# The last two result tiles of a routed mixture of experts: turned by TensorE and stored as whole rows

## The chip, the cores and the metric

The kernel runs on one core of one Trainium2 chip. The core has five engines that run at the same time and meet only at semaphores: TensorE (PE in the profile, and PEld for its weight loads), VectorE (DVE), ScalarE (ACT), GpSimd (POOL) and SyncE (SP). SP computes nothing; it issues DMAs. ACT can issue DMAs too. The DMAs of both queues run on the core's 16 DMA engines. The metric is the device time of one execution in microseconds, lower is better. A time is given as the median over several executions.

## The reference

Two blocks in a row. The first is an attention with a polynomial sketch (4 batches, 4 heads, 1088 positions, 32 dimensions for each head); its output, heads side by side, is the matrix x of 4352 tokens by 128 features. The second sends x through 8 experts, and its result is a weighted sum over all of them:

```
logits = x @ w_gate
P = np.exp(logits - logits.max())
for _ in range(8):
    P /= P.sum(1, keepdims=True) + 1e-09
    P /= P.sum(0, keepdims=True) + 1e-09
    P *= N / E
for e in range(E):
    h = np.maximum(x @ w1[e], 0.0)     # 128 -> 1024 features
    out += P[:, e:e + 1] * (h @ w2[e]) # 1024 -> 128 features
```

Everything is float32. The output has 4352 rows of 128 numbers, 512 bytes for each token.

## The kernel before

Features lie on the 128 partitions and tokens along the columns, so xT holds x turned round. The columns are not in the order of the tokens: each batch has 34 blocks of 32 columns, and column 32a + s of a batch is token 34s + a. Blocks that follow each other in the columns are therefore rows that follow each other in the output, and the 32 columns of one block are rows that lie 34 rows apart.

The expert part is cut into groups of tokens (`groups`, L644 to L653) and, in a group, into items, one for each expert. TensorE makes the hidden features of 256 tokens at a time (`first`, L920), ScalarE applies the maximum with zero, and TensorE multiplies by w2 (`into`, L1092), into four PSUM banks that the program names s. To spare products, blocks of w2 and of the hidden features are added and subtracted beforehand, so that a bank holds no finished output; finished tiles come from sums of banks, which VectorE makes (`part_of_seven`, `part_of_twenty`, and `last_part` for the last group).

The last group is `(0, 256, 2, [2..7], True)`: two tiles of 256 tokens, columns 0 to 511 of batch 0. `last_part` (L795) is called when a bank of this group is complete, in the order 3, 0, 2, 1. Bank 2 completes the tile y2 (columns 256 to 511), bank 1, the last, completes the tile y1 (columns 0 to 255). From two blocks before the end on, the order on VectorE, TensorE and ScalarE is the order in which the program issues the instructions (`manual_schedule`, L1126). The products of bank 1 are the last ones on TensorE.

A finished tile has features on partitions and tokens in columns, and the output wants tokens in rows. `put` (L723) has VectorE transpose the tile in squares of 32 by 32 (L726). Partition 32r + s of the result holds, for every block of the tile, the 32 features of quarter r of one token. `store` (L878) then issues four DMAs, one for each quarter r; each writes 32 times 8 pieces of 32 numbers, which are 128 bytes, a quarter of a row (L884). In the last group the four alternate between the queues of SP and ACT:

```
            for r in range(4):
                queues[r % len(queues)].dma_start(
                    out=AP(tensor=out.tensor, offset=out[b * S + a, 32 * r].offset,
                           ap=[[SA * DM, 32], [DM, m], [1, 32]]),
                    in_=yt[32 * r:32 * (r + 1), b0 - first:b0 - first + m, :])
```

All other groups store by `put` as well, with SP alone, in the middle of the program. Other names that matter here: `bank()` (L94) gives one of four PSUM banks named a, which `first` uses; `ident` (L286) is the 128 by 128 identity in SBUF, which `routing` (L597) and `kept_to_sums` (L1060) use as an operand; L630 stores the routing weights, four DMAs of 8 rows each, into a DRAM tensor pT; L191 loads w2 in pieces of 512 bytes; line L1280 is where the program ends and the engines meet.

Of the kernel before, what the change touches and what calls it, by code (L numbers as in the profile page):

```python
# [10 lines left out]
F32 = mybir.dt.float32  # L11
# [39 lines left out]
def kernel(  # L51
# [12 lines left out]
    nc = tc.nc  # L64
    P = nc.NUM_PARTITIONS
    B, H, S, D = q.shape
    R = S1.shape[0]
    N, DM = out.shape
# [3 lines left out]
    SA = S // 32  # L72
# [6 lines left out]
    H2 = DM // 2  # L79
# [14 lines left out]
    def bank():  # L94
        return aps.tile([P, 512], F32, tag="a", name="a")
# [61 lines left out]
    loaded, pools = {}, []  # L157
# [128 lines left out]
    ident = consts.tile([P, P], F32, name="ident")  # L286
# [436 lines left out]
    def put(y, lo, n, queues):  # L723
        b0, nb = lo // 32, n // 32
        yt = pools[0].tile([P, NT3 // 32, 32], F32, tag="yt", name="yt", bufs=4)[:, 0:nb, :]
        nc.vector.transpose(out=yt.rearrange("p b d -> p (b d)"), in_=y)  # L726
        store(yt, b0, b0 + nb, queues)

    def part(g, k):

        if g in DIRECT:
            lo, n, _, es, _ = groups[g]
            nc.scalar.copy(kept[es[0]][:, lo + k * n:lo + (k + 1) * n], sums[g][k])
        elif groups[g][2] == 3:
            part_of_twenty(g, k)
        elif g < len(groups) - 1:
            part_of_seven(g, k)
        else:
            last_part(g, k)
# [47 lines left out]
    def last_rooms(g):  # L787
        n = groups[g][1]
        own = parts.setdefault(g, {})
        if not own:  # L790
            own.update(y=[pools[0].tile([P, NT3], F32, name=f"y{t}", bufs=1)[:, 0:n] for t in range(2)],
                       **{a: room(a, n) for a in "zwxfr"})
        return [own[a] for a in "yzwxfr"]

    def last_part(g, k):  # L795


        lo, n, *_ = groups[g]
        s0, s1, s2, s3 = sums[g]

        def add(out, a, b):
            nc.vector.tensor_tensor(out, a, b, op=Alu.add)

        (y1, y2), z, w, x, f, r = last_rooms(g)
        if k == 3:
            nc.scalar.copy(r[upper], s3[lower])
            add(w[upper], s3[upper], r[upper])
        elif k == 0:
            nc.scalar.copy(z[upper], s0[lower])
            nc.scalar.copy(f, s0)  # L810
            add(x[upper], z[upper], w[upper])
            add(z[upper], x[upper], s0[upper])
        elif k == 2:
            nc.scalar.copy(r[lower], s2[upper])
            nc.scalar.copy(x[lower], s0[lower])
            add(y2[upper], z[upper], s2[upper])
            add(y2[lower], s2[lower], r[lower])
            add(x[upper], x[upper], s2[upper])
            put(y2, lo + n, n, (nc.sync, nc.scalar))
        else:  # L820
            add(y1, s1, x)
            put(y1, lo, n, (nc.sync, nc.scalar))

    def part_of_twenty(g, k):

# [52 lines left out]
    def store(yt, b0, b1, queues):  # L878
        first = b0
        while b0 < b1:  # L880
            b, a = divmod(b0, SA)
            m = min(b1 - b0, SA - a)
# [5 lines that stand above are left out]
            b0 += m  # L888
# [396 lines left out]
```

## Time and profile before

| what | us |
|---|---|
| median of 6 runs | 920.09 (919.62 to 921.14) |
| the profiled execution | 919.79 |
| its span, first to last instruction | 918.0 |
| PE busy in the span | 911.1 (99%) |
| DVE busy | 689.3 (75%) |
| ACT busy | 421.2 (46%) |
| POOL busy | 211.9 (23%) |
| last matmul begins and ends its group | 911.07 to 913.00 |
| last DMA issue begins, on SP and on ACT | 914.92 and 914.96 |

The profile is one execution. The rows of a timeline give the start in microseconds from the span's start, how long the row took, the engine, the line of the program, the operation with its tiles (out<-in) and shapes, and how many instructions are merged in the row. An engine name with a q at its end (SPq, ACTq) is that engine's queue, where DMAs are issued. The row of an issue is over before the data move. In a table of stretches, "DMA share" is the mean busy share of the 16 DMA engines, from the time that their packets took, and can be over 1 where packets of one engine overlap. A DMA has one packet for each contiguous piece that it moves, and beside these some packets of 4 bytes, here called marks, that tell the semaphore that a part has landed; each of the last eight stores has 256 packets and 16 marks.

### The profile page before, as it was taken

The page shows a single profiled execution, that of the slowest core. Times are in us where ns is not written, and L with a number is a line of the kernel's source. Part 1 is how long each engine was busy: PE and PEld are TensorE (multiplying, and loading weights), DVE is VectorE, ACT ScalarE, POOL GpSimd, SP SyncE. Part 2 cuts the span into 40 slices and gives each one's busy share as a digit, 9 for nine tenths or more (in the row PEclk, how much of TensorE's full clock was granted, in tenths as well). Part 3 has the DMA queues.
Part 4 walks back from the last instruction along what each step waited for, and adds up shares of the span by engine and source line. Part 5 has one row for each costly group of instructions (what it writes and reads, how often), then busy time and mean ns, then how long its engine had stood idle before and what let it go on. Part 6 is the DMA issues. An engine that isn't in the chain of part 4 may idle for free.

```text
span 918.0 us, 18917 instructions
## 1 busy us (share of the span) xinstructions
PE 911.1 (99%) x7450; PEld 594.6 (65%) x7450; DVE 689.3 (75%) x1173; ACT 421.2 (46%) x915; POOL 211.9 (23%) x220
## 2 busy tenths in 40 slices
PE   9999999999999999999999999999999999999997
PEld 7877544466666666666666666666666655556886
DVE  8678699888877798766975666966567976658665
ACT  3455555554444454444544444544445444445443
POOL 5121100175555421201210010110100243211220
PEclk9999999999999999999999999999999999999999
DMA  9994100214453535434363343453334455453640
GB/s 260 315 269 155 54 1 1 70 64 140 144 162 119 187 119 172 166 110 150 114 186 132 119 141 112 134 186 128 132 123 165 131 169 196 161 166 93 173 155 13
DMA packets 91305, 128.15 MB, mean 140 GB/s; under 512 B 25392, under 2 KB 69504, under 8 KB 86480
## 3 DMA queue, kind: packets, MB, share of 16 engines
q1 hardware_dynamic: 88384, 121.42, 41.9%
q0 software_dynamic: 1600, 5.36, 1.9%
q8 instruction: 58, 0.95, 0.4%
q10 hardware_dynamic: 1232, 0.16, 0.1%
q14 instruction: 31, 0.25, 0.1%
HBM read 107.88 MB, written 19.05 MB: 138 GB/s over the span
## 4 chain that ended last, share of the span: by engine, by line
PE 98%; DVE 1%; issue 0%; ACT 0%; POOL 0%; DVEq 0%; POOLq 0%
PE a L926 56%; PE s L1111 38%; PE a L352 1%; PE a L474 1%; PE a L114 1%; PE a L319 0%; DVE hb L943 0%; PE s L381 0%; PE a L438 0%; PE s L404 0%; PE a L508 0%; PE a L387 0%; PE a L404 0%; DVE cs L614 0%; DVE rs L608 0%
## 5 line engine op out<-in xcount | busy, mean ns | idle before, releaser
L926 PE MATMUL a<-xe,w 128*64 128x256 f32 (+1 forms) x2560 | 663.3, 470 | 0.0
L926 PEld LDWEIGHTS a<-xe,w 128*64 128x64 f32 x2560 | 300.7, 137 | 105.8 <-issue 1.6
L1111 PE MATMUL s<-hb,ws 128*64 128x256 f32 (+3 forms) x1312 | 314.0, 395 | 0.2 <-DVE hb L943 0.2
L930 ACT ACTIVATE hb<-a 128x256 f32<-128x256 f32 (+4 forms) x408 | 194.8, 480 | 242.0 <-PE a L926 209.0
L1111 PE MATMUL s<-hx,ws 128*64 128x256 f32 x1280 | 289.2, 379 | 0.0
L930 ACT ACTIVATE hx<-a 128x256 f32<-128x256 f32 (+1 forms) x360 | 167.1, 464 | 213.7 <-PE a L926 193.9
L990 DVE TENSOR_TENSOR hb<-hb 128x512 f32<-128x512 f32 (+1 forms) x204 | 139.4, 693 | 97.9 <-ACT hb L930 93.8
L990 DVE TENSOR_TENSOR hx<-hx 128x512 f32<-128x512 f32 (+1 forms) x204 | 154.8, 769 | 60.6 <-ACT hx L930 55.4
L1111 PEld LDWEIGHTS s<-hb,ws 128*64 128x64 f32 x1312 | 148.7, 137 | 77.6 <-issue 26.1
L690 POOL TENSOR_TENSOR xe<-xT,xe 128x768 f32<-128x768 f32 (+2 forms) x41 | 82.5, 2014 | 480.6 <-DMA xe<-pT 398.5
L1111 PEld LDWEIGHTS s<-hx,ws 128*64 128x64 f32 x1280 | 145.8, 137 | 62.4 <-issue 13.4
L1111 PE MATMUL s<-hb,w 128*64 128x256 f32 (+3 forms) x536 | 129.0, 408 | 0.0
L926 PE MATMUL a<-xT,w 128*64 128x416 f32 (+3 forms) x512 | 120.2, 462 | 0.0
L1111 PE MATMUL s<-hx,w 128*64 128x256 f32 x384 | 90.4, 379 | 0.0
L943 DVE TENSOR_TENSOR hb<-hb 128x416 f32<-128x416 f32 (+7 forms) x84 | 60.2, 717 | 20.5 <-ACT hb L930 16.6
L1111 PEld LDWEIGHTS s<-hb,w 128*64 128x64 f32 x536 | 57.9, 137 | 23.4 <-issue 6.6
L926 PEld LDWEIGHTS a<-xT,w 128*64 128x64 f32 x512 | 50.1, 137 | 24.3 <-issue 15.3
L242 POOL TENSOR_TENSOR ws<-w 128x256 f32<-128x256 f32 (+1 forms) x70 | 63.3, 938 | 5.8 <-DMA w<-in_moe_w_dram 4.4
L943 DVE TENSOR_TENSOR hx<-hx 128x256 f32<-128x256 f32 (+1 forms) x65 | 39.5, 612 | 24.3 <-ACT hx L930 23.1
L1111 PEld LDWEIGHTS s<-hx,w 128*64 128x64 f32 x384 | 44.1, 137 | 11.4
L990 DVE TENSOR_TENSOR pqg<-hb 128x512 f32<-128x512 f32 x68 | 45.3, 708 | 0.0
L990 DVE TENSOR_TENSOR pqg<-hx 128x512 f32<-128x512 f32 x68 | 34.7, 551 | 0.0
(184 smaller groups left out, 485.2 us busy)
## 6 DMA issues: line engine op xcount, KB each, us to landing
w<-in_moe_w_dram SPq DMA_DIRECT2D x82, 512.0 KB, 5.5
ws<-ws SPq DMA_DIRECT2D x34, 1024.0 KB, 5.0
xe<-pT SPq DMA_DIRECT2D x34, 384.0 KB, 3.9
ws<-ws SPq DMA_DIRECT2D x12, 512.0 KB, 4.0
ph<-qa SPq DMA_DIRECT2D x12, 288.0 KB, 4.9
rb<-qb SPq DMA_DIRECT2D x3, 1152.0 KB, 6.5
pb<-pT SPq DMA_DIRECT2D x6, 384.0 KB, 7.5
kx<-in_k_dram SPq DMA_DIRECT2D x4, 544.0 KB, 4.0
```

What stands on the lines that cost most here:

```text
L114: nc.tensor.matmul(warm[:, 0:P], ones, ones, start=True, stop=True)
L242: tc.keep_in_program_order(nc.gpsimd.tensor_tensor(ws[:, c:c + len(ns)], blocks(x), blocks(y), op=Alu.subtract if off else Alu.add))
L352: nc.tensor.matmul(pv[64 * s:64 * (s + 1), i], kp[0:n, H * t + h].rearrange("p i j -> p (i j)"), vx[0:n, slots[h], t, :], start=(t == 0 an ...
L474: nc.tensor.matmul(pn[64 * s:64 * (s + 1), t, 2 * i:2 * i + 2].rearrange("p h d -> p (h d)"), ph[:, i, s, 64 * t:64 * (t + 1)], kvs[b % 2] ...
L690: tc.keep_in_program_order(nc.gpsimd.tensor_tensor(out, x, pb, op=Alu.mult))
L926: nc.tensor.matmul(ph[sl], loaded_w[j][0][:, P * f + H2 * s:P * f + H2 * (s + 1)], sources[j][:, lo:hi], start=True, stop=True, tile_posit ...
L930: nc.scalar.activation(out=out, in_=ph, func=Act.Relu)
L943: nc.vector.tensor_tensor(out, a, b, op=Alu.subtract)
L990: nc.vector.tensor_tensor(out if not isinstance(out, tuple) else places(*out), places(*a), places(*b) if isinstance(b, tuple) else b, op=A ...
L1111: nc.tensor.matmul(sums[g][i][H2 * s:H2 * (s + 1), n * place:n * (place + 1)], w, x, start=c == 1, stop=c == per, tile_position=(0, H2 * s))
```

## The change

In `last_part`, bank 2 no longer calls `put` for y2. When bank 1 is complete, y1 is added in two halves of 128 columns. Then each of the four pieces of 128 tokens (two of y2, two of y1) is turned by TensorE: the piece is the stationary operand, 64 columns at a time, the identity is the moving operand, and the two products fill a 128 by 128 corner of a PSUM bank with tokens on partitions and all 128 features along the columns. ScalarE copies the pieces of y2 to SBUF, VectorE those of y1. Four DMAs, alternating between SP and ACT, write 128 rows of 512 bytes each. Their output pattern counts, from the slowest to the fastest, 4 blocks, 32 rows that lie 34 rows apart, and 128 numbers.

```
--- before.py
+++ after.py
@@ -816,10 +816,27 @@
             add(y2[upper], z[upper], s2[upper])
             add(y2[lower], s2[lower], r[lower])
             add(x[upper], x[upper], s2[upper])
-            put(y2, lo + n, n, (nc.sync, nc.scalar))
         else:
-            add(y1, s1, x)
-            put(y1, lo, n, (nc.sync, nc.scalar))
+
+            rows = [slice(P * i, P * (i + 1)) for i in range(n // P)]
+            for c in rows:
+                add(y1[:, c], s1[:, c], x[:, c])
+            work_ = [(y, first_ + c.start, y[:, c]) for y, first_ in ((y2, lo + n), (y1, lo)) for c in rows]
+            turned_ = []
+            for _, _, y in work_:
+                pt = bank()[:, 0:P]
+                for i in range(2):
+                    sl = slice(H2 * i, H2 * (i + 1))
+                    nc.tensor.matmul(pt[sl], y[:, sl], ident, start=True, stop=True, tile_position=(0, H2 * i))
+                turned_.append(pt)
+            for i, (y, token, _) in enumerate(work_):
+                yt = pools[0].tile([P, P], F32, name=f"row{i}", bufs=1)
+                (nc.scalar.copy if y is y2 else nc.vector.tensor_copy)(yt, turned_[i])
+                b, a = divmod(token // 32, SA)
+                (nc.sync, nc.scalar)[i % 2].dma_start(
+                    out=AP(tensor=out.tensor, offset=out[b * S + a, 0].offset,
+                           ap=[[DM, P // 32], [SA * DM, 32], [1, DM]]),
+                    in_=yt)
```

## The prediction

> **What bounds the kernel now.** First the page's busy times and the chain that ended last: TensorE is busy all the time, so all but the last few microseconds are its own work, which the change leaves alone.
>
> ```profile
> span 918.0 us, 18917 instructions
> PE 98%; DVE 1%; issue 0%; ACT 0%; POOL 0%; DVEq 0%; POOLq 0%
> ```
>
> So only the end matters, and there I read the timeline, from the last products on:
>
> ```profile
> 911.07 1.93 PE L1111 MATMUL s<-hb,w 128*64 128x256 f32 x15
> ...
> 912.15 0.42 DVE L802 TENSOR_TENSOR y<-s,r 64x256 f32<-64x256 f32 x1
> 912.60 0.42 DVE L802 TENSOR_TENSOR x<-x,s 64x256 f32<-64x256 f32 x1
> 913.05 0.45 DVE L726 STREAM_TRANSPOSE yt<-y 128x256 f32<-128x256 f32 x1
> 913.52 1.84 SPq L884 DMA_DIRECT2D out_dram<-yt  x4
> 913.53 0.42 DVE L802 TENSOR_TENSOR y<-s,x 128x256 f32<-128x256 f32 x1
> 913.53 1.91 ACTq L884 DMA_DIRECT2D out_dram<-yt  x4
> 913.99 0.45 DVE L726 STREAM_TRANSPOSE yt<-y 128x256 f32<-128x256 f32 x1
> ```
>
> The reader is to see that computing is over at 914.44, and that the first stores are issued at 913.52. The other 3.6 us are DMA. The table of short stretches shows of what kind:
>
> ```profile
> 914.30:914.40 0.10, 0.00 (x0) 0.00 (x0) 0.10 (x1) 0.00 (x0) 0.00 (x0) 1.00 0.10 15
> 914.50:915.00 0.50, 0.00 (x0) 0.00 (x0) 0.00 (x0) 0.00 (x0) 0.00 (x0) 1.00 0.91 133
> 915.50:916.00 0.50, 0.00 (x0) 0.00 (x0) 0.00 (x0) 0.00 (x0) 0.00 (x0) 1.00 0.90 132
> 916.40:916.50 0.10, 0.00 (x0) 0.00 (x0) 0.00 (x0) 0.00 (x0) 0.00 (x0) 1.00 0.18 23
> ```
>
> The last two columns are the DMA share and GB/s. Data begin at 914.38, some 0.86 us after the first issue, and all 16 engines are about 0.9 busy until 916.5. The stores queue at the engines: the end is set by the first issue, 0.86 us, the time the engines need for all packets, and about 1.5 us from the last packet to the end of the span at 918.0 (the last marks land, SP sees them, the engines meet). Each term is judged by this.
>
> **The change part by part.** *Taken away:* two transposes on DVE (2 x 0.45 us), eight issues (0.34 to 0.47 us each), and 2048 packets of 128 bytes. In place of them come 512 packets of 512 bytes.
>
> *Added for y2.* y2 is ready at 912.57, but TensorE runs in order and ends its last products at 913.00. A product of the same shape stands in `routing`:
>
> ```profile
> L597 PE MATMUL a<-ident,mx x4: 272/272/273, 114.4 to 115.2; 128*64 128x128 f32 x4
> L810 ACT COPY f<-s 128x256 f32<-128x256 f32 x1 | 0.4, 372 | 0.0
> L830 ACT COPY z<-s 128x512 f32<-128x512 f32 x5 | 2.9, 583 | 0.0
> ```
>
> A pair runs side by side on two halves of the array, so the first piece is in PSUM by 913.27. A copy of 128 columns on ACT takes half the step from 512 to 256 columns less than 372 ns: 372 - 106 = 266 ns, so 913.55. The first issue on SP is then at about 913.57, today 913.52. I take the start of data as unchanged, 914.4. The second copy puts the first ACT issue at 913.85.
>
> *Added for y1.* With the transpose of y2 gone, the addition starts at 913.05. DVE takes 0.42 us for 256 columns and 0.69 us for 512 (the subtractions of hx just before the end), so 0.29 us for 128: halves at 913.34 and 913.66. Then 0.14 us of weight load, 0.27 us of product and 0.29 us of copy: the last issue, on ACT, at 914.45. The granted clock is 1.00 here. The new waits (PE for DVE, ACT and DVE for PE, the queues for the copies) have nothing queued behind them but the next piece and the program's end. All four stores are at the DMA engines by 915.3, so nothing of this shows as long as the engines are then still working off earlier stores; where they are not, it is the path, as in the rival with 16 engines.
>
> *The stores.* Here I differ from what the packet sizes alone suggest. How many engines a store uses can be read where a store has few rows. L630 writes four times 8 rows; the stretch from 171.2 to 174.0 has it:
>
> ```profile
> DMA packets 57, 0.15 MB, mean 53 GB/s; under 512 B 24, under 2 KB 24, under 8 KB 56
> q1 hardware_dynamic: 56, 0.14, 36.1%
> pT<-qT SPq DMA_DIRECT2D x4, 34.0 KB
> ```
>
> 56 packets are 4 x 8 rows and 24 marks of 4 bytes. Three stores had ended, so each left 8 marks and ran on 8 engines. Today's final stores, whose slowest dimension counts 32, leave 2176 packets, which is 8 x (256 + 16): all 16 engines. The new pattern counts 4 in its slowest dimension on the DRAM side, against 128 partitions on the other. No row here has two sides that differ below 16; the bounds are 4 engines and 16. I take 4, by the pT rows, in which the slowest dimension set the number.
>
> [...]
>
> *Pace.* On 4 engines each store is 32 packets for one engine, and all four go to the same engines one after the other: in the pT stretch four separate bursts follow each other too. For a packet of 512 bytes the loads of w2 are the nearest rows (stretches 820 to 825 and 822.5 to 823.0):
>
> ```profile
> q1 hardware_dynamic: 1040, 0.52, 38.5%
> ...
> q1 hardware_dynamic: 341, 0.17, 115.1%
> ```
>
> The first gives 0.385 x 5 us x 16 / 1040 = 30 ns a packet, the second, at full flow, 0.5 us x 16 / 341 = 23.5 ns from one packet to the next: the lower end. The upper end is pT again: 0.361 x 2.8 x 16 / 32 = 0.50 us a packet of 4352 bytes, where a load of k (0.956 x 0.6 x 16 / 50, from 3.5 to 4.1) took 0.18 us. Few engines on neighbouring partitions cost 2.7 times there, which would be 80 ns. I take 30 / 0.9 = 33 ns, since today's stores keep an engine 0.9 busy: near the lower end, because the new stores read all 128 partitions, not 8 adjacent ones.
>
> [...]
>
> *Sum.* 4 stores x (32 x 33 ns + 10 ns for a mark) = 4.26 us. Start 914.4 + 4.26 + 1.5 = 920.16, against 918.0: **+2.1 us**. The profiled execution (919.79) would be 921.9. The median of the six runs stands 0.3 above it, so I forecast 920.09 + 2.1 = **922.2 us**. At 23.5 ns it is 914.4 + 3.05 + 1.5 = 918.95 (+0.9), at 80 ns 914.4 + 10.3 + 1.5 = 926.2 (+8.2).
>
> **The rivals.** A measurement of this kernel tells about 0.2%, or 1.84 us, from no change; 4 engines cross that bound at 31 ns a packet.
>
> *Four engines, faster packets (23 to 31 ns).* +0.9 to +1.8 us, time about 921.4. For it: the flow of 23.5 ns in a stretch with 16 engines. Against it: the slow packets of pT, and today's 0.9.
>
> *Sixteen engines.* If the 128 partitions decide, the last issue at 914.45 sets the end: data at 915.31, 8 packets of 33 ns and a mark, 0.27 us, end of data 915.58, plus 1.5 gives 917.08: -0.9 us, time 919.2. From 8 engines up the time is not above today's (914.4 + 512 x 33 ns / 8 + 0.04 + 1.5 = 918.05). For it: the source has 128 rows, and every other DMA here runs on 16. Against it: pT.
>
> *Four engines that stand in each other's way as with pT.* 60 to 80 ns: +5.6 to +8.2 us, time about 927. Against it: pT's 8 engines read 8 adjacent partitions.
>
> **How the numbers follow.** The forecast (31 to 45 ns, +1.9 to +3.7) 0.58; faster packets 0.27; sixteen engines 0.10; pT's slowness 0.05. The forecast and the faster packets together run from 921.0 to 923.8. The range 920.8 to 924.0 adds 0.2 at each end for the spread between runs and leaves out the last two rivals. Slower by over 0.2%: 0.58 + 0.05 = 0.63. Within: 0.27, and 0.08 of sixteen engines: 0.35. Faster: 0.02, if sixteen engines come with a shorter tail too.
>
> **What would show it.** In the profile after, the first new issue should stand at 913.6 and the last by 914.5; the share of the DMA engines should be near 0.25 for 4 us, ending near 918.6; 512 packets of 512 bytes should come with 4 marks for each store, 528 in all. A share near 1 for a fraction of a microsecond and 576 packets would be the sixteen engines. A first issue later than 914 would mean that I mispriced products or copies. I am also wrong if anything ahead of 911 moves, since the last products should end where they do now.

## The result and the profile after

The changed kernel takes 922.67 us (median of 16 runs, 921.54 to 924.37) against 920.15 us for the kernel before (36 runs): 1.0027 times as long, with a 95% interval of 1.0020 to 1.0034. That is 2.5 us more, between 1.8 and 3.1. Forecast were 922.2 us, in a range of 920.8 to 924.0. The profiled execution took 921.62 us, with a span of 919.7.

TensorE's own work did not move. Its last products of the experts end at 912.77 in this profile, which answers to the row at 911.07 of before. The end of the timeline (start and duration in us, queue or engine, line, operation, tiles):

```profile
910.68 2.09 PE L1128 MATMUL s<-hb,w 128*64 128x256 f32 x16
911.92 0.42 DVE L802 TENSOR_TENSOR y<-s,r 64x256 f32<-64x256 f32 x1
912.37 0.42 DVE L802 TENSOR_TENSOR x<-x,s 64x256 f32<-64x256 f32 x1
912.49 1.51 PE L830 MATMUL a<-ident,y 128*64 128x128 f32 x16
912.93 0.49 DVE L802 TENSOR_TENSOR y<-s,x 128x128 f32<-128x128 f32 x2
913.05 0.48 ACT L834 COPY row<-a 128x128 f32<-128x128 f32 x2 [1.20 <-PE a L830]
913.34 1.33 SPq L836 DMA_DIRECT2D out_dram<-row  x2
913.56 1.95 ACTq L836 DMA_DIRECT2D out_dram<-row  x2
913.76 0.57 DVE L834 COPY row<-a 128x128 f32<-128x128 f32 x2 [0.34 <-PE a L830]
```

The first store is issued 0.57 us after the last product (913.34 - 912.77), where it was 0.52 before (913.52 - 913.00). Products, copies and additions cost what was forecast: 0.27 us for a product, 0.265 for a copy on ACT, 0.29 for one on DVE and 0.29 for an addition of 128 columns. Note that the queues are slower: two issues on ACT take 1.95 us, while four took 1.91 before. The first of the two takes 1.30 us, so the last store is issued only at 914.96.

The stretches after that (the last two columns are the share of the 16 DMA engines and GB/s):

```profile
914.00:914.50 0.50, 0.00 (x1) 0.00 (x0) 0.33 (x2) 0.00 (x0) 0.00 (x0) 1.00 0.00 0
914.50:915.00 0.50, 0.00 (x0) 0.00 (x0) 0.00 (x0) 0.00 (x0) 0.00 (x0) 1.00 0.16 34
915.00:915.50 0.50, 0.00 (x0) 0.00 (x0) 0.00 (x0) 0.00 (x0) 0.00 (x0) 1.00 0.29 84
916.50:917.00 0.50, 0.00 (x0) 0.00 (x0) 0.00 (x0) 0.00 (x0) 0.00 (x0) 1.00 0.29 85
917.50:918.00 0.50, 0.00 (x0) 0.00 (x0) 0.00 (x0) 0.00 (x0) 0.00 (x0) 0.50 0.25 76
918.00:918.50 0.50, 0.00 (x0) 0.00 (x0) 0.00 (x0) 0.00 (x0) 0.00 (x0) 0.50 0.01 2
```

and the DMA totals from 914 to 919:

```profile
DMA packets 528, 0.26 MB, mean 52 GB/s; under 512 B 16, under 2 KB 528, under 8 KB 528
```

Where 16 engines were 0.9 busy for 2.1 us, about 4 of 16 are busy for 3.4 us (0.29 and not 0.25: 479 of the 512 packets take 27 ns, but in the full stretches the next one on an engine begins after 24, so they overlap a little). The 16 packets under 512 bytes are the marks: four for each of four stores. So the stores run on 4 engines, and on the same 4: the share stays near 0.29 while stores of both queues are under way, and their data follow each other (SP from 914.65 and from 916.33, ACT from 915.51 and from 917.13), though SP's second store was issued at 914.10.

How the tails compare is seen best from the last product on, because the part ahead of it differs by up to a microsecond from one execution to the next (its end lies between 912.8 and 913.9 in all the profiles below, the kernel's own 913.0). All times are from one profile each, read off the timeline and the stretches:

| kernel | products end | first issue | first data | last data | span ends | products to end |
|---|---|---|---|---|---|---|
| before | 913.00 | 913.52 | 914.38 | 916.5 | 918.0 | 5.0 |
| changed | 912.77 | 913.34 | 914.65 | 918.1 | 919.7 | 7.0 |
| changed, second profile | 913.57 | 914.13 | 915.44 | 918.8 | 920.4 | 6.9 |
| changed, third profile | 913.57 | 914.13 | 915.44 | 919.0 | 920.6 | 7.1 |
| e3, 2 engines | 913.48 | 914.04 | 915.33 | 922.2 | 923.6 | 10.1 |
| e2, 8 engines | 913.58 | 914.36 | 915.72 | 918.0 | 919.3 | 5.8 |
| e1, 16 engines | 913.11 | 913.99 | 915.24 | 917.7 | 919.7 | 6.6 |
| e6, 16 engines, 4 products | 913.40 | 914.29 | 915.55 | 917.1 | 918.8 | 5.4 |
| e9, 16 engines, reads with steps | 913.55 | 914.41 | 915.65 | 917.2 | 918.9 | 5.4 |
| e7, rows that follow each other | 913.84 | 914.40 | 915.24 | 916.6 | 918.3 | 4.5 |
| e8, changed, 4 products | 913.79 | 914.54 | 915.84 | 919.3 | 921.0 | 7.2 |
| e11, changed, shorter at the start | 913.42 | 913.99 | 915.30 | 918.8 | 920.5 | 7.0 |
| e5, before and 8 idle products | 913.60 | 914.12 | 914.97 | 918.3 | 920.3 | 6.7 |
| e10, before, y2 stored earlier | 913.21 | 913.28 | 914.13 | 916.7 | 918.2 | 5.0 |

The tail of the changed kernel is 1.9 to 2.1 us longer, in three profiles. The medians of the times differ by 2.5. The rest lies outside the span (see e8 and e11).

### The profile page after: what moved, and what is told of

Same layout as the page of the kernel before. It is cut to its first block, busy times and chain, and to the rows that moved or that the text cites. A ratio compares the mean times of both kernels' runs of the same rounds, so it can differ in the third digit from the quotient of the medians.

```text
span 919.7 us, 18945 instructions
## 1 busy us (share of the span) xinstructions
PE 912.1 (99%) x7466; PEld 692.4 (75%) x7466; DVE 689.4 (75%) x1174; ACT 421.8 (46%) x917; POOL 215.9 (23%) x220
## 4 chain that ended last, share of the span: by engine, by line
PE 98%; DVE 1%; issue 0%; ACT 0%; POOL 0%; DVEq 0%; POOLq 0%
PE a L943 55%; PE s L1128 38%; PE a L352 1%; PE a L474 1%; PE a L114 1%; PE a L319 0%; DVE hb L960 0%; PE s L381 0%; PE a L438 0%; PE s L404 0%; PE a L508 0%; PE a L387 0%; PE a L404 0%; DVE cs L614 0%; DVE rs L608 0%
## 5 line engine op out<-in xcount | busy, mean ns | idle before, releaser
L943 PEld LDWEIGHTS a<-xe,w 128*64 128x64 f32 x2560 | 304.6, 137 | 73.0 <-issue 1.6
L1128 PE MATMUL s<-hb,ws 128*64 128x256 f32 (+3 forms) x1312 | 300.1, 395 | 0.2 <-DVE hb L960 0.2
L1128 PE MATMUL s<-hx,ws 128*64 128x256 f32 x1280 | 275.1, 379 | 0.0
L1007 DVE TENSOR_TENSOR hx<-hx 128x512 f32<-128x512 f32 (+1 forms) x204 | 158.0, 785 | 59.9 <-ACT hx L947 54.5
L1128 PEld LDWEIGHTS s<-hb,ws 128*64 128x64 f32 x1312 | 162.8, 137 | 50.2 <-issue 14.7
L690 POOL TENSOR_TENSOR xe<-xT,xe 128x768 f32<-128x768 f32 (+2 forms) x41 | 84.8, 2069 | 476.4 <-DMA xe<-pT 364.6
L1128 PEld LDWEIGHTS s<-hx,ws 128*64 128x64 f32 x1280 | 158.9, 137 | 37.7
L1128 PE MATMUL s<-hb,w 128*64 128x256 f32 (+3 forms) x536 | 127.1, 408 | 0.0
L1128 PE MATMUL s<-hx,w 128*64 128x256 f32 x384 | 88.3, 379 | 0.0
L1128 PEld LDWEIGHTS s<-hb,w 128*64 128x64 f32 x536 | 60.1, 137 | 17.1 <-issue 6.6
```

What stands on the lines that cost most here:

```text
L690: tc.keep_in_program_order(nc.gpsimd.tensor_tensor(out, x, pb, op=Alu.mult))
L943: nc.tensor.matmul(ph[sl], loaded_w[j][0][:, P * f + H2 * s:P * f + H2 * (s + 1)], sources[j][:, lo:hi], start=True, stop=True, tile_posit ...
L1007: nc.vector.tensor_tensor(out if not isinstance(out, tuple) else places(*out), places(*a), places(*b) if isinstance(b, tuple) else b, op=A ...
L1128: nc.tensor.matmul(sums[g][i][H2 * s:H2 * (s + 1), n * place:n * (place + 1)], w, x, start=c == 1, stop=c == per, tile_position=(0, H2 * s))
```

## The experiments

**The theory** is that of the prediction: a store runs on as many DMA engines as its slowest dimension allows, and four stores in one row on four engines are the loss. **The rival** is that turning by TensorE and storing whole rows costs the time by itself, on any number of engines.

### e1: 16 engines

The additions that make y2 and y1 write their columns in another order, so that the stores can count the 32 positions of a block first:

```
+            tokens = lambda t: t.rearrange("p (c a s) -> p c a s", c=2, a=4)
+            rows_ = lambda t: t.rearrange("p (c s a) -> p c s a", c=2, a=4)
-            add(y2[upper], z[upper], s2[upper])
+            add(rows_(y2[upper]), tokens(z[upper]), tokens(s2[upper]))
...
-                           ap=[[DM, P // 32], [SA * DM, 32], [1, DM]]),
+                           ap=[[SA * DM, 32], [DM, P // 32], [1, DM]]),
```

> The changed kernel with the columns of y2 and y1 written in the order (position in the block, block), so that the four stores count 32 in their slowest dimension instead of 4. Products, copies and number and size of the pieces stay. Theory (a store runs on as many engines as its slowest dimension allows, 4 before and 16 here): data of the last store from about 915.3 for 0.3 us, end 917.0 in the span, about 919.2 us, which is 1 us below the kernel before and 3.4 below the changed one; 528 packets become 576. Rival (the products, copies and whole rows themselves cost the time, whatever the engines): 922.7 us as the changed kernel. If writing columns with a step costs VectorE, it shows as rows over 0.42 us at the additions.

Measured: 921.33 us, 1.0011 times the kernel before (1.0002 to 1.0019). The stores do run on 16 engines, as the totals from 914 on show, 64 marks for four stores:

```profile
DMA packets 577, 0.28 MB, mean 29 GB/s; under 512 B 64, under 2 KB 576, under 8 KB 576
q8 instruction: 1, 0.02, 0.6%
```

That takes back 1.3 us of the 2.5, so the rival does not hold for the whole. But 919.2 us was expected: 2.1 us are missing. Three things are seen. The additions to y2 took 0.63 and 0.61 us instead of 0.42. The first data came 1.25 us after the issue, not 0.86. And the second line is a packet that is no data: 16 KB of program code. It came at 915.69 and took 0.88 us. Most packets of the stores had ended by 916.8; the last 27 went on until 917.68 at a DMA share of 0.05 to 0.08, about one engine of 16. It fits that they had queued behind the code on its engine.

### e2: 8 engines

One store for each tile; stationary operands take every second column:

```
+                    x_ = y.rearrange("p (a s j) -> p j a s", s=16, j=2)[:, j]
...
+                           ap=[[DM, n // 32], [SA * DM, 32], [1, DM]]),
```

> One store for each tile, 8 blocks of 32 rows: slowest dimension 8, each of 8 engines has 32 packets of each of two stores. Theory: 64 packets for an engine instead of 128; last issue 914.4, 1.3 us to the first packet as in the changed kernel's first store, 0.8 us of packets, 1.6 to the end: 918.1 in the span, about 920.2 us. Packets 512 + 16. Rival (engines do not matter): 922 to 922.7 us.

Measured: 921.40 us, 1.0012 times (1.0003 to 1.0021). 16 marks for two stores: 8 engines. The sum was too low by 1.2 us; the queues' rows of the timeline show part of it:

```profile
914.36 0.73 SPq L839 DMA_DIRECT2D out_dram<-row  x1
915.29 1.20 ACTq L839 DMA_DIRECT2D out_dram<-row  x1
```

The store of y1 waits for both of its pieces and is issued only at 915.29, 1.7 us after the products; expected was 1.4. What the rest of the 1.2 us is was not tried.

### e3: 2 engines

```
+                for h in range(2):
+                    (nc.sync, nc.scalar)[i % 2].dma_start(
+                        out=AP(tensor=out.tensor, offset=out[b * S + a + 2 * h, 0].offset,
+                               ap=[[DM, 2], [SA * DM, 32], [1, DM]]),
+                        in_=yt[H2 * h:H2 * (h + 1)])
```

> Two stores for each piece of 128 rows, 2 blocks of 32 rows each: slowest dimension 2, eight stores. Theory: 256 packets for each of 2 engines at 23.5 to 27 ns, 6.0 to 6.9 us against 3.4: 2.6 to 3.5 us above the changed kernel, 925.3 to 926.2 us; 512 + 16 packets at a DMA share of 0.13. Rival (engines do not matter): 922.7 us, at most 0.9 more for four more issues on two queues.

Measured: 925.87 us, 1.0063 times (1.0051 to 1.0076), inside what the theory gave. One of its stretches:

```profile
919.00:919.50 0.50, 0.00 (x0) 0.00 (x0) 0.00 (x0) 0.00 (x0) 0.00 (x0) 0.50 0.14 43
```

and the totals from 914 on, 16 marks for eight stores:

```profile
DMA packets 529, 0.28 MB, mean 29 GB/s; under 512 B 16, under 2 KB 528, under 8 KB 528
```

Two of 16 engines, at 43 GB/s, half of the 84 of the changed kernel. Data take 915.33 to 922.15, 6.8 us, against 3.4 on four engines: 26.6 and 26.8 ns a packet (6.82 us / 256 and 3.43 us / 128). The number of engines sets the length, as the theory has it. A block of code came at 916.17 here too, among the stores; until 918.4 the pace is 30 to 31 ns a packet, after that 24.

### e4 and e12: the changed kernel again

> The changed kernel once more, for a second profile and the same chip as the three others: 922.7 us by the result. The profiled execution showed a span only 1.7 us longer than before, the medians 2.5 us; if the profile was a fast draw, its second span should come out at 920 to 921 and differ from the first in the start of the data or in their pace, not ahead of 911 us.

> The changed kernel a third time, as partner for the one with 10 products of ones: 922.7 us, with one code block behind the end of the span and a device time 1.9 to 2.7 us over it.

Measured: 922.87 and 922.68 us. The tails are the same in all three profiles. Their products end at 913.57 instead of 912.77: the difference is ahead of the tail, not in it, against what e4's text expected. One block of code comes behind the end of the span each time, at 920.67, 922.21 and 921.63. The executions took 1.89, 2.66 and 1.78 us more than their spans, so the 1.9 to 2.7 of e12's text fails too.

### e5: only the code of the eight products

The kernel before, and after all else:

```
+            for c in range(4):
+                pt = bank()[:, 0:P]
+                for i in range(2):
+                    sl = slice(H2 * i, H2 * (i + 1))
+                    nc.tensor.matmul(pt[sl], ident[:, sl], ident, start=True, stop=True, tile_position=(0, H2 * i))
```

> The kernel before with eight products of the identity with itself added on TensorE after all else, as many as the change adds, into PSUM banks that nothing reads. Theory (the longer program of TensorE costs, because one more block of its code is loaded, 59 instead of 58 packets of 16 KB): 59 such packets, the last near the end or behind it, and 920.3 to 921.1 us. Rival (code costs nothing): 58 or 59, and 920.2 us, within 0.1% of the kernel before.

Measured: 921.26 us, 1.0009 times (1.0001 to 1.0018), 1.15 us more, though nothing waits for the products. The page has one block of code more than the 58 of before, and the stretches show how the stores went with it:

```profile
q8 instruction: 59, 0.97, 0.4%
```

```profile
915.00:915.50 0.50, 0.00 (x0) 0.00 (x0) 0.03 (x1) 0.00 (x0) 0.00 (x0) 1.00 1.02 158
916.00:916.50 0.50, 0.00 (x0) 0.00 (x0) 0.00 (x0) 0.00 (x0) 0.00 (x0) 1.00 0.81 119
917.00:917.50 0.50, 0.00 (x0) 0.00 (x0) 0.00 (x0) 0.00 (x0) 0.00 (x0) 0.50 0.10 9
917.50:918.00 0.50, 0.00 (x0) 0.00 (x0) 0.00 (x0) 0.00 (x0) 0.00 (x0) 0.50 0.44 67
918.00:918.50 0.50, 0.00 (x0) 0.00 (x0) 0.00 (x0) 0.00 (x0) 0.00 (x0) 0.50 0.50 69
```

The block begins at 915.47 and takes 1.33 us. From 916.5 on hardly any data move, and those that were held back finish at 918.3, where 917.1 would answer to the kernel before (its 3.5 us from products to last data). What held them back shows in the queues. The last issue on each took four times as long as before (0.45 and 0.47 us):

```profile
915.51 1.71 SPq L889 DMA_DIRECT2D out_dram<-yt  x1
915.56 1.67 ACTq L889 DMA_DIRECT2D out_dram<-yt  x1
```

Of the 576 pieces that move after 916.6, most are those of these two stores (512). So here, with a block of code among the last stores, whole stores came late, and not only packets on about one engine as in e1. This profile is the slowest of 11 runs. Three others took 920.0 to 920.2 us, no more than the kernel before, and the interval leaves 0.1 to 1.7 us.

### e6: 16 engines and less code

```
-                for i in range(2):
-                    sl = slice(H2 * i, H2 * (i + 1))
-                    nc.tensor.matmul(pt[sl], y[:, sl], ident, start=True, stop=True, tile_position=(0, H2 * i))
+                nc.tensor.matmul(pt, y, ident, start=True, stop=True)
```

> The 16-engine version with four products of all 128 columns instead of eight of 64, so 8 matmul rows fewer for TensorE. Theory (the code block is what held one DMA engine back in the 16-engine version, from 915.69 for 0.88 us, so that its packets ended 0.9 us after all others): if the block is not loaded, or later, all packets end by 916.8 and the time is about 920.4 us. Rival (sixteen engines are no faster here): 921.3 us again.

Measured: 920.57 us, 1.0005 times (0.9997 to 1.0014), as the theory had it within 0.2 us. No block of code comes after 914, and all data are over at 917.1. With the block, e1's late packets are gone too. The totals from 914 to 918:

```profile
DMA packets 576, 0.26 MB, mean 66 GB/s; under 512 B 64, under 2 KB 576, under 8 KB 576
```

### e7: all but the pattern

```
-                    out=AP(tensor=out.tensor, offset=out[b * S + a, 0].offset,
-                           ap=[[DM, P // 32], [SA * DM, 32], [1, DM]]),
+                    out=AP(tensor=out.tensor, offset=out[P * i, 0].offset, ap=[[DM, P], [1, DM]]),
```

> The changed kernel, but the four stores write 128 rows that follow each other, so that both sides count 128 in one dimension: the last two tiles land on the wrong rows of the output, all else stays. It measures products, copies and whole rows with a store as simple as that of L209. Theory (the pattern alone is what the change pays for): issues of 0.32 us instead of 0.56 to 1.3, first data 0.85 us after the issue instead of 1.3, 16 engines; last issue 914.4, end 917.1, 919.2 us, up to 920.1 if the code block costs as in the changed kernel. Rival (products and copies themselves cost the time): 921 us and more.

Measured: 919.96 us, 0.9998 times (0.9990 to 1.0007). In the profile its tail is 4.5 us, 0.5 shorter than before. Its queue rows and its busiest stretch:

```profile
914.40 1.08 SPq L836 DMA_DIRECT2D out_dram<-row  x2
914.62 1.14 ACTq L836 DMA_DIRECT2D out_dram<-row  x2
```

```profile
916.00:916.50 0.50, 0.00 (x0) 0.00 (x0) 0.00 (x0) 0.00 (x0) 0.00 (x0) 1.00 0.78 231
```

With the products, copies and whole rows of the changed kernel and a plain pattern, the first data follow the issue by 0.84 us (915.24 - 914.40), and the loss is gone. That ends the rival: the pattern of the stores is what the change pays for. It is 0.8 us above the theory's lower value. This version cannot be had as it is, since the rows of a tile do not follow each other in the output.

### e8 and e11: the changed kernel without the extra block of code

e8 uses four products of 128 columns, as e6 does. e11 leaves the end alone and makes the program shorter at the start:

```
-    for _ in range(14):
+    for _ in range(10):
         nc.tensor.matmul(warm[:, 0:P], ones, ones, start=True, stop=True)
```

> The changed kernel with four products of all 128 columns instead of eight of 64; its stores stay on 4 engines. Theory (part of its 2.5 us is the code block, loaded behind the end of the span in both of its profiles, where the execution took 1.89 and 2.66 us more than the span against 1.78 before): if the block is not loaded, span and time differ by 1.78 us again and the time is about 922.1 us. Rival (the four engines are all of it): 922.7 us again, less 0.1 for the shorter products.

> The changed kernel with 10 instead of 14 products of ones at the start (L113), which nothing reads: TensorE's program is then as much shorter as in the version with products of 128 columns, and its end is untouched. Theory (the code block behind the end costs the changed kernel about 0.6 us): 58 blocks, device time 1.78 us over the span, about 922.1 us. Rival (the block costs nothing): as the changed kernel in the same call, 922.7 us.

Measured: 922.41 us (1.0024 times, 1.0014 to 1.0034) and 922.78 us (1.0028 times, 1.0016 to 1.0040); e12, run beside e11, has 922.68. Neither profile has the extra block, and both executions took 1.8 us more than the span. e8's products take 0.2 us longer to the first issue than the pairs (0.75 against 0.57 us).

The medians of e11 and e12 are level, but they come from six and seven runs that spread over 2.3 and 2.7 us, so they cannot tell 0.6 us. The difference between the time and the span of each run tells more. It is what lies outside the span:

| runs | median of the spans | time less span, lowest to highest | mean |
|---|---|---|---|
| kernel before, 87 | 918.4 | 1.72 to 1.85 | 1.79 |
| changed kernel, 30 | 920.35 | 1.73 to 3.45 | 2.15 |
| e8, 8 | 920.6 | 1.76 to 1.86 | 1.81 |
| e11, 6 | 921.0 | 1.75 to 1.83 | 1.78 |

(The 87 runs are those of the kernel before beside the experiments, the 30 are the first measurement, e4 and e12.) The changed kernel's span is 1.95 us longer, as its tail is. Some 0.4 us more, in the mean, lie outside the span: nothing in some executions, up to 1.6 us in others. Without the extra block this is not seen: time less span is never over 1.86 us in e8 and e11, nor in e6, e9 and e10. e11's own time is no shorter because its six spans came out longer, though its tail is the same (7.0).

In the three profiles of the changed kernel the block ended 2.13, 2.91 and 1.87 us behind the end of the span, and the executions took 1.89, 2.66 and 1.78 us more than the span: the later the block, the later the end. This speaks for the block as the cause, but does not prove it. One kernel does not fit: e7's profile has no such block, and its runs took up to 2.09 us more than their spans. If it is the block, the theory was right in kind, and its 0.6 us was too much.

e8 also gives the price of the engines most closely. e6 has the same products and no extra block, but 16 engines: 920.57 us against 922.41, 1.8 us less, although its additions are slower.

### e9: steps on the reading side

```
-            tokens = lambda t: t.rearrange("p (c a s) -> p c a s", c=2, a=4)
-            rows_ = lambda t: t.rearrange("p (c s a) -> p c a s", c=2, a=4)
+            tokens = lambda t: t.rearrange("p (c a s) -> p c s a", c=2, a=4)
+            rows_ = lambda t: t.rearrange("p (c s a) -> p c s a", c=2, a=4)
...
```

> The 16-engine version with products of 128 columns, in which the additions read with steps and write in order, instead of the other way round. Theory (writing with steps made the additions 0.62 us instead of 0.42 and 0.38 instead of 0.29): rows of 0.42 and 0.29 us, the stores 0.4 us earlier, 920.2 us, level with the kernel before. Rival (VectorE pays for a step on either side): rows of 0.6 us and 920.6 us again.

Measured: 920.71 us, 1.0004 times (0.9995 to 1.0013). The rival was right:

```profile
912.26 0.60 DVE L802 TENSOR_TENSOR y<-z,s 64x256 f32<-64x256 f32 x1 [0.42 <-ACT r L814]
912.88 0.59 DVE L802 TENSOR_TENSOR y<-s,r 64x256 f32<-64x256 f32 x1
```

### e10: y2 stored earlier, in the kernel before

```
-            add(x[upper], x[upper], s2[upper])
             put(y2, lo + n, n, (nc.sync, nc.scalar))
+            add(x[upper], x[upper], s2[upper])
```

> The kernel before with one exchange on VectorE: y2 is transposed and stored ahead of the addition to x, so its stores are issued 0.45 us earlier and y1 keeps its time. Theory (the stores queue at 16 engines that are 0.9 busy from 914.4 to 916.5, so what starts earlier ends earlier): end of data at 916.2 instead of 916.5, about 919.9 us, too little to tell. Rival (the end hangs on y1's issues alone): 920.2 us.

Measured: 920.38 us, 1.0000 times (0.9991 to 1.0009). The first issue comes 0.07 us after the last product instead of 0.52. Those of y1 come after 1.57 us (914.78 - 913.21) instead of 1.46. The end does not move:

```profile
914.50:915.00 0.50, 0.00 (x0) 0.00 (x0) 0.25 (x1) 0.00 (x0) 0.00 (x0) 1.00 0.92 133
915.00:915.50 0.50, 0.00 (x0) 0.00 (x0) 0.00 (x0) 0.00 (x0) 0.00 (x0) 1.00 0.29 40
915.50:916.00 0.50, 0.00 (x0) 0.00 (x0) 0.00 (x0) 0.00 (x0) 0.00 (x0) 0.81 0.65 96
916.00:916.50 0.50, 0.00 (x0) 0.00 (x0) 0.00 (x0) 0.00 (x0) 0.00 (x0) 0.50 0.92 131
```

The share falls to 0.29 between the stores of y2 and those of y1. The end hangs on y1, the rival's answer.

No version beat the kernel before by more than its measurement tells.

## Why the prediction was right

The time, the sign and the cause came out: 922.67 us measured, 922.2 forecast, 4 engines instead of 16. The tail, forecast +2.1, is +1.9 to +2.1 in the profiles. By its own terms, against the first profile after:

- **The first issue and the price of the products, copies and halves**: right. 0.57 us from the last product to the first issue, forecast the same (913.00 to 913.57). The one oddity is that a product counts as two rows of the trace, and the first piece takes 0.5 us in all, which is hidden by overlap with the last products of the experts.
- **The last issue**: wrong, but hidden. It was forecast 1.45 us after the last product (914.45 - 913.00) and came after 2.19 (914.96 - 912.77), because ACT's first issue took 1.30 us. The four engines still had earlier stores to write: from 914.65 to 918.07 their flow never stopped.
- **The number of engines**: right, and the step that carries the result. 16 marks for four stores; with 2, 8 and 32 in the slowest dimension 2, 8 and 16 engines (e3, e2, e1). The smaller side set the number where the two sides of a store differ, 4 against 128, which no row of before could show. Nor does a row of before show that all four stores go to the same engines, which the sum assumed; the share of 0.29 and the stores' data that follow each other showed it.
- **From issue to first data**: too small. I took 0.86 us from the stores of before. It was 1.31 us (914.65 - 913.34): 0.45 us missing, of which 0.32 are in the issue itself (0.67 instead of 0.34 us). It is no matter of the number of engines: e1, e6 and e9 on 16 have 1.24 to 1.26 us, and e7 with its plain pattern 0.84. So it goes with the pattern of two dimensions against 128 partitions.
- **The pace**: too slow. Forecast 33 ns a packet, 4.26 us in all; measured 3.43 us, 26.8 ns, and in the full stretches 512 bytes x 4 engines / 84 GB/s = 24 ns. That is the rival "faster packets", which I gave 0.27. It would have ended at +1.3 us with the other terms as forecast; the late first data made up 0.45 of it. Of the 512 packets, 479 took 27 ns, and 24 took 39 ns or more, 13 of these among the first 32.
- **From the last data to the end**: 1.66 us, forecast 1.5.

So two terms of the sum were mis-sized, by -0.83 us (the pace) and +0.6 us (the late first data and the end), and offset each other. And 0.4 us of the measured loss, in the mean, lie outside the span, for which the sum had no term. The forecast stood on the right mechanism and partly on luck.

Two more points of the prediction were wrong though they did not decide. The rival with 16 engines was priced at 919.2 us. As a real store pattern it came out at 920.6 (e6) and 920.7 (e9), because of the late first data and of additions that cost 0.6 us when their columns are reordered; even with a plain pattern it was 919.96 (e7). And "the end is set by the first issue" is not so for the kernel before: with y2 issued 0.45 us earlier the end stays (e10).

What remains open: why the first data of these stores come late and why ACT's first issue is long; and whether the time outside the span is the work of the extra block of code, as the runs suggest.

## What to carry to other kernels

Count the slowest dimension of a store's output pattern before counting bytes: 2, 4 and 8 in front gave 2, 4 and 8 engines, with 64 or 128 partitions on the other side (e3, the changed kernel, e2). Four DMAs with 512-byte rows lost to eight with 128-byte pieces because 4 stood in front and 12 of 16 DMA engines had nothing to do (a share of 0.29, where it was 0.9). At the end of a program, where nothing hides a store, read the time from issue to data, the number of marks and the share of the engines one by one. And instructions that nobody waits for still cost in e5, where one more block of code was loaded among the last stores (1.15 us in the median, with 0.1 to 1.7 left by the interval).

## What the runs showed of the hardware that was not expected

- A block of code, 16 KB, is one packet of 0.88 to 1.33 us; with eight more products on TensorE there are 59 of them instead of 58 (e5). With one among the last stores, some packets came late on about one engine (e1), or the last issues of both queues took 1.7 us (e5). The kernel before has 58 blocks, with the last at 899.1, well ahead of its stores. Where it comes behind the end of the span, some executions take up to 1.6 us more outside the span (30 runs of the changed kernel); that the block does this is not shown.
- The delay from issue to first data goes with the pattern: 0.84 us for 128 rows in one dimension (e7), 0.86 for 32 x 8 pieces against 32 partitions (before), 1.24 to 1.36 for rows in two dimensions against 64 or 128 partitions (32 x 4 in e1, e6 and e9, 4 x 32 in the changed kernel, 8 x 32 in e2, 2 x 32 in e3).
- The first issue on ACT's queue took 1.20 to 1.31 us for stores on 2, 4 and 8 engines (e3, the changed kernel, e2) and 0.63 on 16 (e1), against 0.39 to 0.47 before. The later ones took 0.53 to 0.70.
- VectorE's addition of 64 x 256 float32 took 0.61 to 0.63 us with a step of 4 numbers between neighbouring columns on the writing side (e1), and 0.59 to 0.60 with a step of 32 on the reading side (e9), instead of 0.42.
